# A decode step of two attention layers and two MLPs on one core: the tile of layer 1's exponentials, split maxima, a power for 1/deviation, and a new written-out order

## Chip, cores and metric

One core of a Trainium2 chip runs the kernel. The time is that of one execution on the device in microseconds (us). The engines are PE (TensorE: matmuls, with PEld for its weight loads), DVE (VectorE), ACT (ScalarE), POOL (GpSimd) and SP (SyncE, which issues the loads here); each works through its own queue in order, and they meet at semaphores.

## What is computed

Eight batch rows, one token each. Attention A reads the last 1024 positions of the caches (16 query heads on 8 key heads of 256), MLP B has 1792 hidden columns; the pair is run twice with the same weights and caches.

```python
def _A_ref(x, k_cache, v_cache, wq, wo):
    W = min(4096, max(256, Sk // 4))                  # 1024
    q = (x @ wq).reshape(B, Sq, Hq, Dh)               # heads first
    k = jnp.repeat(k_cache[:, :, Sk - W:, :], rep, axis=1)
    v = jnp.repeat(v_cache[:, :, Sk - W:, :], rep, axis=1)
    p = _softmax(jnp.einsum("bhqd,bhkd->bhqk", q, k) * Dh ** -0.5, axis=-1)
    o = jnp.einsum("bhqk,bhkd->bhqd", p, v)
    return o.reshape(B, Sq, Hq * Dh) @ wo
def _B_ref(x, w1, w2):
    return jnp.einsum("bsf,fd->bsd", _silu(jnp.einsum("bsd,df->bsf", x, w1)), w2)
x = x + _A_ref(_layernorm(x), ...)     # layer 1
x = x + _B_ref(_layernorm(x), w1, w2)
x = x + _A_ref(_layernorm(x), ...)     # layer 2, same wq, wo and caches
x = x + _B_ref(_layernorm(x), w1, w2)
```

## The kernel before

**Loads.** The weights are loaded once and stay. K and V pass through `ring`, 30 slots of one key head of one batch row (0.52 MB, loaded as two half slots of 256 KB). A row takes 16 slots, 8 of K and 8 of V, and both layers use them while they are there: layer 2 of a row needs what layer 1 and the MLP made of it, so K waits in its slots for layer 2's scores (which free four K slots for each half of the heads), and V for layer 2's products (`pv_rows` with layer 1 as its index). SP issues the loads in the order of the rows, each when its slot is free and at most ten ahead (`load_k` L713, `load_v` L719).

**One row, layer 1** (`layer1(b)`). DVE transposes the 16 half slots of K in place (L1246, called K transposes here). `q_blocks1` (L858, ACT) writes the row's queries into the tile `qbd[0]` as blocks with zeros between them, so that one matmul serves several heads. `scores` (L881) multiplies K by them into a PSUM bank; `softmax` takes the maximum (L892, DVE), turns it over the partitions (L900 to L905), and ACT makes exponentials with it as a bias (L912) into `e_sb`; PE transposes them (L918, ACT evicts at L927), sums them (L931), multiplies V (`pv_rows`, L951) into two banks for heads 0 to 7 and 8 to 15, of which ACT evicts each (L956) for a transposing matmul (L958) and DVE scales it (L971). One head group of V takes a column form (`pv_cols`, L985). `rows_part` (L1002) multiplies by wo in rows, ACT evicts the sum (L1018) and `fold` (L1019) adds it to the residual columns in bank YB.

**The MLP** (`up`, `chain`). ACT copies the residual to bf16 (L1029, L1030), `stat` (L1036, L1040) sums x and its square, DVE makes the variance (L1046), and `rsqrt` makes 1/deviation from it: a guess from the bits (L749) and two Newton steps (L754 and L760, or L757 to L765). `w1_rows` (L842) multiplies by w1, DVE transposes the result (L851) and subtracts the mean (L1063, `vt`), ACT makes the tanh (L1071, `th`), DVE the other factor (L1072, `zh`) and the product `hT` (L1074). w2 follows, by rows (L1002) and, for chunks from `nr` on, by columns (`cols_part`, L1008).

**Layer 2** (`chain`, `layer2(b)`). wq is multiplied in rows (L1104), DVE transposes that (L1109), PE selects heads and positions (L1115, called the selection), DVE adds the mean's share (L1121) and multiplies by a mask into `qbd[1]` (L1129), once for each half of the heads. Layer 2's `stat` hands its variance (L1051, ACT) to nine small POOL instructions (L749 to L765). Then come scores, softmax and V as in layer 1, while layer 1 of the next row runs in between. All of layer 2's outputs meet in `final` (from L1141), a second MLP for all eight rows at once.

**The order.** Each operation is recorded as a task with what it reads and writes. `best_schedule` runs a list scheduler with a model of durations, adds fixed offsets to the tasks' ranks (`OFFSETS`), runs it again and then moves single tasks by a table (`MOVES`). The scheduler also puts `fill` tasks into PE's gaps: matmuls of zeros by 512 columns (L1290) which change nothing. `PAIR0 = 1` lets layer 1's scores take both halves of the heads in one matmul of 512 columns, `NR2 = 14` sends all of w2 by rows (in the last row 8 chunks by rows), and `WQS = 0` keeps the first wq product in one bank (in the last row it goes to two).

**Tiles that the change touches.** `e_sb[0]`, `e_sb[1]`, `rowb`, `yT` and `o_sb[0]` all lie in the tile `qT`, which also takes the q transposes: layer 1's exponentials of a row cannot be written before the selection of the row before has read `qT`. The columns of `rowb` behind the 448 are zeroed by POOL in each row (L1257).

Of the kernel before, what the change touches and what calls it, by code (L numbers as in the profile page):

```python
# [1 line left out]

# [12 lines left out]
SEM_LAT = {"pe": 0.05, "dve": 0.05, "act": 0.05, "pool": 0.08, "sp": 0.1}  # L15
LAT = {"pe": 0.17, "dve": 0.07, "act": 0.09, "pool": 0.08, "sp": 0.0}
SWITCH = 0.1
FETCH = (128, 1.4, 0.26)
WINDOW, WARM, ACTIVE, PACED = 3.413, 43.0, 3072.0, 50.0
FIRST, LANDED = 1.2, 1.5  # L20
HOLDS = (("PVc0", 1, "oTc0", 1), ("s12", 1, "hT", 1), ("wq", 2, "qbd", 1))
HELD = ("KT", "max0")
OFFSETS = (
# [26 lines left out]
)  # L50
LOOKS = (0.3, 0.15)

MOVES = {
# [1275 lines left out]
```

## Time and profile before

| | us |
|---|---|
| three runs: median (lowest, highest) | 241.06 (241.04, 242.05) |
| the profiled execution: span from first to last instruction | 239.7 |
| what the median has over that span | 1.36 |
| PE busy, all matmuls; of this fillers (L1290, 129 matmuls) | 194.1; 38.6 |
| DVE busy; of this K transposes (L1246, 128) | 152.8; 81.4 |
| ACT busy; POOL busy | 86.5; 26.0 |
| last stretch, 206 us to the end: DMA | 4 GB/s |

The profile is of one execution, and durations are from it. A line of the groups gives line, engine, operation, out<-in, count, then busy time, mean of one in ns, and the idle time of the engine just before them with what ended it. A line of the timeline gives start, length, engine, line and operation. In the chain of waits each piece has its start and the time that it alone held the end up. "x16" behind a matmul is a count.

### The profile page before, as it was taken

Reading aid. Unit: us, or ns where it says so; the run is one execution under the profiler, and the core shown is the slowest. Engines: PE = TensorE matmul, PEld = TensorE weight load, DVE = VectorE, ACT = ScalarE, POOL = GpSimd, SP = SyncE. Lnnn points to the kernel's source line nnn. Section 1 sums busy time; section 2 is a strip of 40 time slices with the busy share of each in tenths; the row PEclk is TensorE's granted clock in tenths of the full one; section 3 lists DMA queues with packets and bytes.
Section 4 is the critical chain, followed back from the end, with each engine's and each line's share of the span. In section 5 each row is a group of like instructions: output and inputs, shape, how many; then the busy total and the mean of one; then the engine's idle time right before and its main releaser. Section 6 shows DMA issues by size and latency. Waiting matters only on the chain.

```text
span 239.7 us, 8472 instructions
## 1 busy us (share of the span) xinstructions
PE 194.1 (81%) x3567; PEld 97.3 (41%) x3567; DVE 152.8 (64%) x425; ACT 86.5 (36%) x292; POOL 26.0 (11%) x125
## 2 busy tenths in 40 slices
PE   1052358878989899989898898989898999899894
PEld 1051123232345344535433453454344535445552
DVE  7339620037955995996599669946985996334533
ACT  2001231033045516532734354355416440544331
POOL 6100000002010031004001200310031003003000
PEclk9999985999999999999999999999999999999999
DMA  6999999999999999999999999999999999200000
GB/s 228 373 355 403 404 402 384 378 374 406 402 405 403 403 402 404 398 350 379 360 400 402 371 373 379 376 368 377 358 399 399 397 330 399 102 3 3 4 3 1
DMA packets 40341, 78.22 MB, mean 326 GB/s; under 512 B 4320, under 2 KB 6512, under 8 KB 39792
## 3 DMA queue, kind: packets, MB, share of 16 engines
q1 hardware_dynamic: 40304, 77.69, 87.2%
q8 instruction: 28, 0.46, 0.7%
q14 instruction: 9, 0.07, 0.1%
HBM read 77.67 MB, written 0.01 MB: 324 GB/s over the span
## 4 chain that ended last, share of the span: by engine, by line
PE 47%; DMA 19%; DVE 16%; ACT 7%; SPq 7%; issue 4%; POOL 0%; DVEq 0%; ACTq 0%
DMA ring<-in_A_k_cache_dram 10%; PE bank L951 9%; PE bank L881 7%; DMA w2o<-in_B_w_dram 6%; DVE ring L1246 6%; PE bank L1002 6%; PE bank L1290 5%; PE bank L1104 5%; PE bank L1115 3%; DMA ring<-in_A_v_cache_dram 3%; SPq L682 3%; ACT qT L912 2%; DVE mrow L892 2%; PE bank L918 2%; PE bank L958 1%
## 5 line engine op out<-in xcount | busy, mean ns | idle before, releaser
L1246 DVE STREAM_TRANSPOSE ring<-ring 128x512 uint32<-128x512 uint32 x128 | 81.4, 684 | 10.7 <-DMA ring<-in_A_k_cache_dram 10.7
L1290 PE MATMUL bank<-wq_sb,smalls 128*128 128x512 bf16 x129 | 38.6, 386 | 0.0
L881 PE MATMUL bank<-ring,qbd 128*16 128x512 bf16 (+2 forms) x768 | 35.8, 324 | 3.4 <-DVE ring L1246 2.3
L951 PE MATMUL bank<-ring,pT_sb 128*4 128x512 bf16 (+1 forms) x512 | 36.2, 378 | 0.1
L881 PEld LDWEIGHTS bank<-ring,qbd 128*16 128x16 bf16 (+1 forms) x768 | 19.6, 91 | 17.1 <-DVE qbd L1129 3.9
L858 ACT ACTIVATE qbd<-q1s 32x128 bf16<-32x128 bf16 x32 | 10.2, 320 | 42.9 <-PE bank L881 42.3
L892 DVE TENSOR_REDUCE mrow<-bank 128x2 f32<-128x512 f32 (+1 forms) x17 | 11.0, 646 | 11.9 <-PE bank L881 11.1
L1104 PE MATMUL bank<-wq_sb,xn 128*4 128x512 bf16 (+1 forms) x272 | 17.7, 369 | 0.9 <-ACT x2s L1091 0.5
L1018 ACT ACTIVATE qT<-bank 128x448 bf16<-128x448 f32 x16 | 8.7, 543 | 22.4 <-PE bank L1002 22.4
L951 PEld LDWEIGHTS bank<-ring,pT_sb 128*4 128x4 bf16 (+1 forms) x512 | 11.5, 84 | 11.1 <-issue 1.8
L1290 PEld LDWEIGHTS bank<-wq_sb,smalls 128*128 128x128 bf16 x129 | 10.2, 98 | 12.3 <-issue 7.6
L918 PE MATMUL bank<-ident,qT 128*64 128x16 bf16 x256 | 8.5, 180 | 7.3 <-ACT qT L912 6.6
L1002 PE MATMUL bank<-w2o,oT 128*1 128x448 bf16 x224 | 13.2, 352 | 0.7 <-DMA w2o<-in_A_wo_dram 0.7
L956 ACT ACTIVATE qT<-bank 128x512 bf16<-128x512 f32 x16 | 9.6, 597 | 9.7 <-PE bank L951 6.7
L1109 DVE STREAM_TRANSPOSE qT<-bank 128x512 f32<-128x512 f32 (+1 forms) x17 | 11.3, 664 | 2.2 <-PE bank L1104 2.0
L918 PEld LDWEIGHTS bank<-ident,qT 128*64 128x64 bf16 x256 | 6.1, 111 | 12.5 <-ACT qT L912 11.5
L956 ACT ACTIVATE qbd<-bank 128x512 bf16<-128x512 f32 (+1 forms) x16 | 9.1, 570 | 5.5 <-PE bank L951 3.3
L749 POOL TENSOR_SCALAR smalls<-smalls 128x1 int32<-128x1 int32 x8 | 1.5, 190 | 86.9 <-ACT smalls L1051 76.3
L1257 POOL MEMSET qT<- 128x64 bf16 x8 | 1.2, 152 | 82.5 <-PE bank L958 68.7
L1115 PE MATMUL bank<-qT,w2o 128*32 128x64 f32 x128 | 8.4, 352 | 2.0 <-DVE qT L1109 0.8
L912 ACT ACTIVATE qT<-bank,mrow 128x256 bf16<-128x256 f32 x17 | 7.2, 470 | 7.6 <-DVE mrow L905 7.3
L1046 DVE SCALAR_TENSOR_TENSOR smalls<-bank,smalls 128x1 f32<-128x1 f32 x8 | 1.1, 143 | 13.2 <-ACT smalls L1044 9.5
(183 smaller groups left out, 254.6 us busy)
## 6 DMA issues: line engine op xcount, KB each, us to landing
ring<-in_A_k_cache_dram SPq DMA_DIRECT2D x128, 256.0 KB, 6.2
ring<-in_A_v_cache_dram SPq DMA_DIRECT2D x128, 256.0 KB, 6.1
w2o<-in_A_wo_dram SPq DMA_DIRECT2D x2, 1792.0 KB, 13.1
wq_sb<-in_A_wq_dram SPq DMA_DIRECT2D x3, 1024.0 KB, 6.8
w2o<-in_B_w_dram SPq DMA_DIRECT2D x1, 1568.0 KB, 14.5
w_sb<-in_B_w_dram SPq DMA_DIRECT2D x3, 448.0 KB, 12.2
wq_sb<-in_A_wq_dram SPq DMA_DIRECT2D x2, 256.0 KB, 10.2
w_sb<-in_B_w_dram SPq DMA_DIRECT2D x2, 112.0 KB, 11.4
```

Source lines behind the costliest of these rows:

```text
L881: fns.append(lambda e, cb=cb, par=par, j=j, kv=kv, m=m, c0=c0, c1=c1: e.matmul(bank[sc][32 * j:32 * j + m, c0:c1], qbd[layer][:, j * 8 + c ...
L892: dve(lambda e: e.tensor_reduce(mseg[layer][:, ks[0]:ks[-1] + 1], bank[sc][:, lo:hi].rearrange("p (k n) -> p k n", k=len(ks)), AX.X, ALU.m ...
L912: act(lambda e, k2=k2: e.activation(e_sb[ei][:, k2, :, :].rearrange("p uh (jj ul) -> p uh jj ul", ul=2), bank[sc][:, k2 * 256:(k2 + 1) * 2 ...
L918: pe([lambda e, uh=uh, ql=ql, k2=k2: e.matmul(bank[lb][64 * ql:64 * ql + 64, k2 * 64:k2 * 64 + 64].rearrange("p (j q u r) -> p u j q r", j ...
L951: fns.append(lambda e, qh=qh, uh=uh, j=j, vv=vv: e.matmul(bank[ob][32 * j:32 * j + 2 * w, 0:w * DH], p_col(ei, k2, j, qh, uh, w), vv, star ...
L956: act(lambda e: e.activation(o_sb[oi][:, 0:w * DH], bank[ob][:, 0:w * DH], ACTF.Copy), bk(ob), O_K[oi], 0.2 + w * 0.2, "oevh" if ob == OB[ ...
L1002: pe([lambda e, i=i, c=c: e.matmul(bank[XB][32 * c:32 * c + 1, 0:D], rhs(i), w_sb[:, i * D:(i + 1) * D], start=(first and i - i0 < 4), sto ...
L1104: fns.append(lambda e, j=j, c=c, wb=wb, off=off, h0=h0, n=n, k2=k2: e.matmul(bank[wb][32 * j:32 * j + 4, h0:h0 + n], xn[:, part(c, k2), j, :],
L1109: dve(lambda e, wb=wb, h0=h0, n=n: e.transpose(qT[:, h0:h0 + n].rearrange("p (c a i) -> p c a i", a=2, i=32), bank[wb][:, h0:h0 + n].rearr ...
L1115: pe([lambda e, qs=qs, j=j: e.matmul(qs[32 * j:32 * j + 32].rearrange("p (k c r) -> p k r c", k=4, c=8), irep, qT[:].rearrange("p (r c i) ...
L1246: dve(lambda e, v=v: e.transpose(v, v), [("slot", s, h)], [("slot", s, h)], 0.67, "KT")
L1290: fills = {n: [lambda e, j=j, m=P // n: e.matmul(bank[OB[0]][m * j:m * j + m, 0:2 * DH], zero_b.broadcast_to([P, m]), wq_sb[:, 0:2 * DH], ...
```

## The change

1. `e_sb[0]` and `o_sb[0]` move from `qT` to `qbd[0]`, layer 1's own query tile. POOL zeroes it in each row but the last, behind the zeroing of `rowb`, and ACT writes the next row's queries after that.
2. Layer 1's maximum is taken for each half of the heads by itself, and its scores too (`PAIR0 = 0`): 64 matmuls of 256 columns a row in place of 32 of 512.
3. 1/deviation of each row's two layer norms is one POOL instruction, variance to the power -0.5; the variance changes its sign and loses the factor of the Newton steps. Layer 2's variance is made on DVE in place of ACT. `zh` moves from DVE to POOL. The Newton steps stay at the start and in `final`.
4. `NR2 = 8`: 6 chunks of w2 go by columns in every row. `WQS = 1`: the first wq product goes to two banks by halves in every row. The second query addition uses `pT_sb[1]` as its buffer (in the last row `mrow[0]` as before).
5. The scheduler, its tables and its model are gone; `ORDER` holds each engine's order as numbers of tasks, with fillers as f1, f2 and f4 (that many matmuls; f2 and f4 use 64 or 32 columns of the array each). 50 filler matmuls in 17 places are left of 129.

```diff
-    NJ, PAIR0, PAIR1, NR2, WQS = 3, 1, 0, 14, 0
+    NJ, PAIR0, PAIR1, NR2, WQS = 3, 0, 0, 8, 1
...
-    e_sb = [qT[:, 256 * i:256 * i + 256].bitcast(BF16).rearrange("p (k u x) -> p k u x", k=2, u=4) for i in range(2)]
+    e_sb = [t.rearrange("p (k u x) -> p k u x", k=2, u=4) for t in (
+        qbd[0][:].rearrange("p n k x -> p (n k x)"), qT[:, 256:512].bitcast(BF16))]
+    QB1 = [("qbq", 0, q) for q in range(4)]
...
-    o_sb = [qT[:, 0:256].bitcast(BF16), qbd[1][:].rearrange("p n k x -> p (n k x)")]
+    o_sb = [q[:].rearrange("p n k x -> p (n k x)") for q in qbd]
...
+    mhalf = smalls[:, 14:15]
...
-        row_max(layer, ks, sc)
+        for k in ((0,), (1,)) if layer == 0 else (ks,):
+            row_max(layer, k, sc)
...
-            dve(lambda e: e.scalar_tensor_tensor(out=va, in0=t2, scalar=-kk / D, in1=m2, op0=ALU.mult,
-                                                 op1=ALU.add), bk(bi) + ["m2"], [("va", si)], 0.16, "va")
+            dve(lambda e: e.scalar_tensor_tensor(out=va, in0=t2, scalar=kk / D, in1=m2, op0=ALU.mult,
+                                                 op1=ALU.subtract), bk(bi) + ["m2"], [("va", si)], 0.16, "va")
...
-            act(lambda e: e.activation(va, t2, ACTF.Identity, bias=m2[:, 0:1], scale=-kk / D), bk(bi) + ["m2"],
-                [("va", si)], 0.26, "va")
-        rsqrt(dve if si == 0 else pool, va, rstd, nt, ("va", si), ("rstd", si), [])
+        pool(lambda e: e.tensor_tensor(rstd, va, mhalf, ALU.pow), [("va", si), "mhalf"], [("rstd", si)], 0.54, "pow")
...
-        dve(lambda e: e.tensor_scalar(zh[:], vt[:], rstds[0][:, 0:1], None, op0=ALU.mult), ["vt", ("rstd", 0)],
-            ["zh"], 0.234, "zh")
+        pool(lambda e: e.tensor_scalar(zh[:], vt[:], rstds[0][:, 0:1], None, op0=ALU.mult), ["vt", ("rstd", 0)],
+             ["zh"], 0.25, "zh")
...
+        if b < NB - 1:
+            pool(lambda e: e.memset(qbd[0][:], 0.0), [], QB1 + [("qbd", 0, 0), ("qbd", 0, 1)], 0.52, "qz")
...
-    pl.best_schedule(fill)
+    pl.arrange(ORDER, fills, "oevh")
```

Three places of the order, each as it was and as it is now. First PE, from row 3's first selection on (before: L1115 is the selection, L1104 the wq product, L881 scores: 8x256 and 16x256 of layer 2 for row 3, 16x512 of layer 1 for row 4, L997 starts row 4's residual):

```order
L1115 MATMUL bank<-qT,w2o 32x4x2x8 x4
L997 MATMUL bank<-xb,ident 128x64
L1104 MATMUL bank<-wq_sb,xn 4x512 x16
L881 MATMUL bank<-ring,qbd 8x256 x32
L1290 MATMUL bank<-wq_sb,smalls 128x512
L881 MATMUL bank<-ring,qbd 16x512 x8
L1115 MATMUL bank<-qT,w2o 32x4x2x8 x4
L881 MATMUL bank<-ring,qbd 16x512 x24
L881 MATMUL bank<-ring,qbd 16x256 x32
```

The same stretch of row 3 now, from its fold (L797) on; L658 are scores, L884 the wq product, L814 and L818 the statistics, L895 the selection:

```order
L797 MATMUL bank<-smalls,qT 128x16 x4
L658 MATMUL bank<-ring,qbd 8x256 x24
L884 MATMUL bank<-wq_sb,xn 4x256 x32
L658 MATMUL bank<-ring,qbd 8x256 x8
L814 MATMUL bank<-xbt 128x32 x4
L818 MATMUL bank<-smalls 128x16
L895 MATMUL bank<-qT,w2o 32x4x2x8 x4
L884 MATMUL bank<-wq_sb,xn 4x512 x16
L658 MATMUL bank<-ring,qbd 8x256 x32
L658 MATMUL bank<-ring,qbd 16x256 x24
L895 MATMUL bank<-qT,w2o 32x4x2x8 x4
L658 MATMUL bank<-ring,qbd 16x256 x8
```

Of layer 1's scores for row 4, 24 + 8 matmuls of the first half stand before the first selection and 24 of the second half before the second one (the 8x256 x32 between are layer 2's of row 3); 8 are left behind it. The statistics have moved behind the halves of the wq product.

Second DVE at the same place, from row 3's first q transpose (L1109) to the maximum (L892), before:

```order
L1109 STREAM_TRANSPOSE qT<-bank 128x512
L1246 STREAM_TRANSPOSE ring<-ring 128x512
L1121 TENSOR_TENSOR mrow<-bank,mrow 128x64
L1129 TENSOR_TENSOR qbd<-mrow,smalls 128x32x8
L1246 STREAM_TRANSPOSE ring<-ring 128x512 x2
L1109 STREAM_TRANSPOSE qT<-bank 128x512
L1121 TENSOR_TENSOR mrow<-bank,mrow 128x64
L892 TENSOR_REDUCE mrow<-bank 128x2
```

And now (L889 q transposes, L829 the variance of layer 2, L1026 K transposes, L901 and L909 addition and mask, L669 the maxima):

```order
L889 STREAM_TRANSPOSE qT<-bank 128x256 x2
L829 SCALAR_TENSOR_TENSOR smalls<-bank,smalls 128x1
L1026 STREAM_TRANSPOSE ring<-ring 128x512
L901 TENSOR_TENSOR mrow<-bank,mrow 128x64
L909 TENSOR_TENSOR qbd<-mrow,smalls 128x32x8
L1026 STREAM_TRANSPOSE ring<-ring 128x512 x2
L889 STREAM_TRANSPOSE qT<-bank 128x512
L901 TENSOR_TENSOR pT_sb<-bank,pT_sb 128x64
L669 TENSOR_REDUCE mrow<-bank 128x1 x2
```

The first q transpose is two halves, a variance has come in, and the maximum is two instructions. In row 6 the two maxima stand behind L909 instead, ahead of the second q transpose.

Third POOL in a row, before (L1257 zeroes the end of `rowb`, L1129 masks the second half of layer 2's queries):

```order
L1257 MEMSET qT 128x64
L749 TENSOR_SCALAR smalls<-smalls 128x1
L757 TENSOR_TENSOR smalls<-smalls 128x1
L758 TENSOR_TENSOR smalls<-smalls 128x1
L763 TENSOR_SCALAR smalls<-smalls 128x1
L765 TENSOR_TENSOR smalls<-smalls 128x1
L757 TENSOR_TENSOR smalls<-smalls 128x1
L758 TENSOR_TENSOR smalls<-smalls 128x1
L763 TENSOR_SCALAR smalls<-smalls 128x1
L765 TENSOR_TENSOR smalls<-smalls 128x1
L1129 TENSOR_TENSOR qbd<-mrow,smalls 128x32x8
```

And now (L1039 zeroes the query tile, L831 are the two powers, L850 is `zh`):

```order
L1037 MEMSET qT 128x64
L1039 MEMSET qbd 128x512
L831 TENSOR_TENSOR smalls<-smalls 128x1
L850 TENSOR_SCALAR zh<-vt,smalls 128x14
L831 TENSOR_TENSOR smalls<-smalls 128x1
L909 TENSOR_TENSOR qbd<-pT_sb,smalls 128x32x8
```

Nine instructions of layer 2's Newton steps have become one power, and the power and `zh` of the MLP between layers have come in ahead of it.

More of the change, by code (lines that the diff above doesn't have):

```diff
@@ new lines, in arrange @@
+    def arrange(self, table, fills, reader):
+        work = [t for t in self.tasks if t.eng != "sp"]
+        loads = [t for t in self.tasks if t.eng == "sp"]
+        self.order = {e: [] for e in ("pe", "dve", "act", "pool")}
+        reads = {}
+        for t in self.tasks:
+            if t.name == reader:
+                reads.update((o.idx, t) for o, _ in t.deps.values() if o.name.startswith("PV0"))
+        for e in self.order:
+            last = None
+            for word in table[e].split():
+                if word[0] == "f":
+                    n, _, after = word[1:].partition("@")
+                    t = Task("pe", fills[int(n)], 0.2, 0.0, "fill")
+                    t.idx, t.sem, t.shape = len(self.tasks), None, (512, int(n))
+                    for k in ("zero_b", ("bank", 2)):
+                        t.deps[self.first_w[k].idx] = (self.first_w[k], True)
+                    if last:
+                        t.deps[last.idx] = (last, False)
+                    if after:
+                        t.deps[loads[int(after)].idx] = (loads[int(after)], True)
+                    self.tasks.append(t)
+                    self.order[e].append(t)
+                    continue
+                lo, _, hi = word.partition("-")
+                for i in range(int(lo), int(hi or lo) + 1):
+                    self.order[e].append(work[i])
+                    last = reads.get(work[i].idx, last)
+        self.order["sp"] = loads
+        assert sum(len(o) for o in self.order.values()) == len(self.tasks)
@@ L861, in q_blocks1 @@
                 [("q1s", t), ("qbd", 0, 0), ("qbd", 0, 1)], [("qbq", 0, q)], 0.3, "qbd1")
-    QB1 = [("qbq", 0, q) for q in range(4)]
     def scores(b, layer, ks, sc):
@@ L924, in softmax @@
                 start=True, stop=True, tile_position=(0, 64 * ql)) for uh in range(4) for ql in range(2)],
[L925 removed]
+               E_K[ei][k2] + ["ident"], bk(lb), (16, 2), "pT%d" % layer)
         k0, k1 = ks[0], ks[-1] + 1
@@ L1129, in chain @@
             (pool if k2 and not tail else dve)(lambda e, dst=dst, qb=qb, mk=mk: e.tensor_tensor(dst, qb, mk, ALU.mult),
-                                               QF + mkey, [("qbd", 1, k2)], 0.55 if k2 and not tail else 0.4, "qbd")
+                                               QF[k2] + mkey, [("qbd", 1, k2)], 0.55 if k2 and not tail else 0.4, "qbd")
     def rows8(banks, n, w_sb, rhs, reads, name):
```

293 lines of the change are left out of this document (30 added, 263 removed), and 89 rows, old and new, of tables (MOVES, OFFSETS, ORDER).

## Prediction

> **What bounds the kernel now.** I read the page first: the span, the rate of the loads over 40 slices, and the chain that ended last.
>
> ```profile
> span 239.7 us, 8472 instructions
> GB/s 228 373 355 403 404 402 384 378 374 406 402 405 403 403 402 404 398 350 379 360 400 402 371 373 379 376 368 377 358 399 399 397 330 399 102 3 3 4 3 1
> PE 47%; DMA 19%; DVE 16%; ACT 7%; SPq 7%; issue 4%; POOL 0%; DVEq 0%; ACTq 0%
> ```
>
> The loads run until slice 34, some 205 us, and 33 us of work follow. They reach 403 to 406 GB/s but do not hold it. The view by stretches of time puts a border on that (columns: stretch, length, busy time of PE, PEld, DVE, ACT and POOL, granted clock, DMA share, GB/s).
>
> ```profile
> 54.00:102.00 48.00, 43.86 (x761) 20.64 (x765) 37.42 (x87) 18.90 (x65) 5.22 (x22) 1.00 1.05 403
> 102.00:196.00 94.00, 85.28 (x1617) 42.03 (x1609) 73.14 (x198) 42.55 (x144) 10.42 (x44) 1.00 1.03 376
> ```
>
> Until 102 us the loads set the pace: a batch row brings 32 half slots of 0.262 MB, 8.39 MB, which at 403 GB/s is **20.8 us a row** (0.65 us a half slot). After 102 us they get only 376 GB/s, since slots of the ring come free late: there the work of a row is the longer. To measure a row I take the transpose behind the w1 product (L851), once a row. The timeline shows it for rows 2, 6 and 7.
>
> ```profile
> 102.89 0.65 DVE L851 STREAM_TRANSPOSE qT<-bank 128x448 f32<-128x448 f32 x1
> 191.98 0.65 DVE L851 STREAM_TRANSPOSE qT<-bank 128x448 f32<-128x448 f32 x1
> 213.15 0.64 DVE L851 STREAM_TRANSPOSE qT<-bank 128x448 f32<-128x448 f32 x1
> ```
>
> Rows 2 to 6 take (191.98 - 102.89) / 4 = **22.27 us** each, row 6 to 7 takes 21.17, and 26.55 us follow to the end. So a row stands 1.5 us over the pace of the loads. Where these go is read from the chain of waits in row 3 (start, length, what):
>
> ```profile
> 126.23 0.92 PE bank L1002 x14
> ...
> 127.79 0.27 PE bank L1019 x4
> ...
> 128.55 1.03 PE bank L1104 x16
> 129.59 0.20 PE bank L1036 x4
> 129.79 0.03 PE bank L1040
> ...
> 130.70 0.53 PE bank L1115 x6
> ...
> 132.33 0.89 PE bank L881 x30
> ...
> 134.08 0.34 PE bank L1115 x4
> 134.42 1.41 PE bank L881 x20
> ...
> 135.85 0.70 DVE mrow L892
> ```
>
> The w2 product, its fold (L1019), the q product (L1104), the selection (L1115), and the scores (L881): behind the second selection stand 1.41 us of layer 1 scores of the next row, which do not need that selection at all, and only then its maximum (L892).
>
> **The change, step by step.** Sizes first: the page of groups has the column form of the w2 product, and the view by source line has both forms of the maximum (minimum, median, longest in ns).
>
> ```profile
> L1008 PE MATMUL bank<-hT,w2o 128*128 128x16 bf16 x24 | 0.7, 170 | 0.0
> L1018 ACT ACTIVATE qT<-bank 128x448 bf16<-128x448 f32 x16 | 8.7, 543 | 22.4 <-PE bank L1002 22.4
> L892 DVE TENSOR_REDUCE mrow<-bank x17: 425/691/693, 31.5 to 224.0; 128x2 f32<-128x512 f32 x15, 128x1 f32<-128x256 f32 x2
> ```
>
> 1. Layer 1 scores come in 64 matmuls of 256 columns instead of 32 of 512, in 8 groups of 8; a group takes 8 x 0.89 / 30 = 0.24. Seven stand ahead of the second selection, one behind. From the selection's end to the end of the maximum it was 1.41 + 0.02 + 0.70 = 2.13. Now the last group lies beside the add on DVE, then two half maxima follow, 0.25 + 2 x 0.425 + two hops of 0.05 = 1.2: **-0.9**.
> 2. The w2 product keeps 8 of 14 chunks as rows, 0.92 x 8 / 14 = 0.53; the other 6 as 24 column matmuls (0.7) lie beside the eviction (0.543). Product to fold was 127.79 - 126.23 = 1.56; now 0.53 + 0.7 + 0.05 = 1.3: **-0.25**.
> 3. Three score groups (0.72) are put between fold and q product, where 128.55 - 128.06 = 0.49 lay open for the copies on ACT: **+0.2**.
> 4. The first q product goes to two banks as halves, so that half the transpose lies beside the second half. Product to selection was 130.70 - 128.55 = 2.15, some of it waiting for DVE; now 1.03, one score group 0.24, the statistics' matmuls (L1036 and L1040) 0.23 and some hops, 1.7: **-0.45**.
>
> Together -1.4, which would make a row 20.9. The second selection I leave where it is: behind the masked queries PE has 32 + 24 score matmuls (1.7), before it had 32, a filler and 8 long ones (134.08 - 132.33 = 1.75).
>
> Powers: POOL takes over 1/deviation. For layer 2 nine POOL instructions become one; for layer 1 five DVE instructions become one on POOL, between the variance (L1046) and the tanh, which waits also for L1063. From the timeline, the layer 2 sequence's ends and the layer 1 slack in row 3:
>
> ```profile
> 123.92 0.16 DVE L1046 SCALAR_TENSOR_TENSOR smalls<-bank,smalls 128x1 f32<-128x1 f32 x1 [0.17 <-PE bank L842]
> 125.31 0.24 DVE L1063 SCALAR_TENSOR_TENSOR vt<-cs,smalls,qT 128x14 f32<-128x14 f32 x1
> 130.65 0.19 POOL L749 TENSOR_SCALAR smalls<-smalls 128x1 int32<-128x1 int32 x1 [10.54 <-ACT x2s L1091]
> 132.96 0.19 POOL L765 TENSOR_TENSOR smalls<-smalls 128x1 f32<-128x1 f32 x1
> ```
>
> No row shows a power. Below it is one POOL instruction on one column, 0.19; above the whole sequence that it replaces, 133.15 - 130.65 = 2.5. The slack is 125.55 - 124.08 = 1.47, less two hops 1.3. I take about 0.5, near the one instruction: cost 0, hidden by the transpose L851. Without that cover each us above 1.3 costs 1 us a row. The product zh goes to POOL beside the tanh.
>
> ```profile
> L1072 DVE TENSOR_SCALAR zh<-vt,smalls 128x14 f32<-128x14 f32 x8 | 1.7, 217 | 0.2
> L1071 ACT ACTIVATE th<-vt,smalls 128x14 f32<-128x14 f32 x8 | 2.5, 307 | 9.0 <-DVE smalls L760 8.8 <-DVE vt L1063 0.2
> ```
>
> It has 0.307 of cover and POOL's small instructions take about 0.2: cost 0. The Trainium skill, GPSIMD Engine Reference, section Key points, calls the vector engine about twice as fast in elementwise work; by that an estimate is 0.43, which would show 0.13 in each of 8 rows, 1.0 us in all; the POOL rows above, as short as DVE's, speak against it at this size.
>
> The query tile of layer 1 now holds exponentials and outputs, so it must be zeroed and rebuilt before the next row's scores:
>
> ```profile
> L626 POOL MEMSET qbd<- 128x512 bf16 x2 | 1.0, 524 | 0.1
> L858 ACT ACTIVATE qbd<-q1s 32x128 bf16<-32x128 bf16 x32 | 10.2, 320 | 42.9 <-PE bank L881 42.3
> 119.95 0.15 POOL L1257 MEMSET qT<- 128x64 bf16 x1 [6.89 <-ACT pT_sb L927]
> ```
>
> The memset follows the one at 119.95, done by 120.7; four copies of 0.32 in gaps of ACT are done by about 124, two to four us before the first scores are asked for (126 to 128). Cost 0; if a copy stands in front of an eviction it costs 0.3. The loads, from DVE's timeline and from the view of waits of SP's queue (waited in all, times, longest):
>
> ```profile
> 95.73 1.35 DVE L1246 STREAM_TRANSPOSE ring<-ring 128x512 uint32<-128x512 uint32 x2 [0.45 <-DMA ring<-in_A_k_cache_dram]
> 98.54 3.67 DVE L1246 STREAM_TRANSPOSE ring<-ring 128x512 uint32<-128x512 uint32 x6
> SPq L719 <- PE bank L881: 8.6, 5, 1.9
> ```
>
> In row 2 nine K transposes stand ahead of L1046 in both orders, and the first waits for its data at 95.73. The ninth lands at 95.73 + 8 x 0.65 = 100.9; with its transpose and the variance, L851 cannot start before 101.75. So all that is gained earlier (the maximum of row 1 need not wait for the first row's second selection) comes to 102.89 - 101.75: **-1.1**.
>
> For rows 2 to 6 I do not take 20.9, on the floor of the loads, but **21.4**: the K transposes wait for loads now, stand in DVE's queue ahead of L851 and the q transposes, and hold them a few tenths a row; layer 2's variance, moved from ACT, stands there too (0.16, as L1046). On PE the early score groups wait for eight of these transposes, and behind them in its queue stand the q product (in rows 4 and 5 the w2 product too), so that a late load now stops the row itself. 4 x (22.27 - 21.4): **-3.5**.
>
> Row 6 to 7: layer 1's maximum of row 7 now stands right behind the first masked query product of row 6, not behind the second.
>
> ```profile
> 198.51 0.42 DVE L1129 TENSOR_TENSOR qbd<-mrow,smalls 128x256 bf16<-128x256 f32 x1
> 202.32 0.69 DVE L892 TENSOR_REDUCE mrow<-bank 128x2 f32<-128x512 f32 x1 [1.05 <-PE bank L881]
> ```
>
> L851 to that product's end was 198.93 - 191.98 = 6.95, less 0.5 of steps 2 to 4, and two half maxima, 0.9: 7.35. From the maximum's end to the next L851 was 213.15 - 203.01 = 10.14; 32 scores of row 6 (1.0) now stand between the two V products, and the last V slots, which SP loads only after the scores of row 6 (the L719 row: longest wait 1.9), I take as 1 us late: 12.2. Sum 19.6 against 21.17: **-1.6**. The tail of 26.55 keeps its chain: 0.
>
> Sum: 239.7 - 1.1 - 3.5 - 1.6 = 233.5. The three runs have a median of 241.06, 1.36 over the span: **234.9 us**.
>
> **Rivals.** (a) The floor: rows at 20.8, 4 x 0.6 less: 232.5. Speaking for it are 403 GB/s until 102 us; against it the queues that now wait for loads. (b) The ring: slots are freed by layer 2's scores, which now end later against the maximum, so rows stay at 22.27 and the first and last terms alone stay: 238.4. (c) The clock. PE's fillers (L1290) fall from 129 matmuls to 50, in 17 places. Early on, before the fillers, the stretches read:
>
> ```profile
> 31.09:34.51 3.42, 0.98 (x25) 0.44 (x18) 1.29 (x4) 2.12 (x7) 0.00 (x0) 1.00 1.05 401
> 34.51:37.92 3.41, 2.71 (x31) 0.93 (x34) 0.43 (x2) 0.86 (x2) 0.00 (x0) 0.50 1.05 397
> 41.33:44.74 3.41, 3.07 (x14) 1.17 (x12) 0.00 (x0) 0.00 (x0) 0.00 (x0) 1.00 1.06 399
> ```
>
> After 3.4 us with PE busy for 0.98 the granted clock is 0.50. If one such stretch a row comes back, PE's 47% of the chain, 1.6 us of it, runs at half speed and loses 0.8: 7 rows, +5.6, 240.5. Against it: scores and V products fill the gaps that fillers filled. The Trainium skill, TensorE: Matmul & The Clock Gate, section What's actually happening, has the clock halved after an idle stretch of some 3.4 us and full again after a busy one, on a window that runs freely; the trace agrees (0.98 of 3.42 busy, then 0.50). (d) Slower: the power is long. At 2.5 us it is 1.2 over the slack, 8 rows, +9.6: 244.5. From 2.1 us on, 0.8 x 8 = 6.4, the gain is gone; beyond 2.2 the kernel is slower.
>
> **How the numbers follow.** Forecast 0.42 (233 to 237.5), (a) 0.18, (b) 0.14, (c) 0.16, (d) 0.07, and 0.03 for a stall that I have not seen, slower. About 0.5% (239.85 to 242.27) can be told from no change. Faster: forecast, (a), (b) and a few hundredths of (c), 0.76. Same: most of (c), 0.12. Slower: (d), the unseen, 0.12 with the bad end of (c). The range, 231 to 241.5, holds (a), (b) and nearly all of (c); it leaves out (d).
>
> **What would show it.** Steps 1 to 4: after 102 us about 392 GB/s (8.39 MB in 21.4), and the transposes behind the w1 product 21.4 apart. Step 1: the half maxima right behind the second add. Powers: POOL's instruction under 1.3 us, and ACT's tanh released by vt, not by POOL. Clock: 1.00 in every slice after 41 us. It is wrong if rows stay over 22, if POOL or DMA releases the tanh or PE's scores, or if the tail grows by more than 0.5.

## The result and the profile after

The changed kernel takes 240.85 us (median of nine runs, 238.94 to 243.51), the kernel before on the same chips 241.51 (nine runs, 241.04 to 242.13). The ratio is 0.9944, with a 95% interval of 0.9917 to 0.9971: a gain of 0.6% where 2.6% was forecast. (Here and below a ratio leaves out runs over 1.5% above the fastest of their kernel, here three of nine; a median does not.) The time forecast, 234.9, was missed by 6 us; the range, 231.0 to 241.5, holds the median.

The profiled execution took 238.94, the fastest of the nine. The traces below explain that one; what the median has above it, 1.9 us, no trace shows. Its page: the span, the granted clock and the load rate over 40 slices, and the chain that ended last, by engine and by line.

```profile
span 237.1 us, 9247 instructions
...
PEclk9999998875699999979999999999999999999997
...
GB/s 224 381 362 402 406 403 386 384 370 406 403 404 402 403 403 400 400 281 360 403 403 349 393 399 363 289 401 403 402 394 399 401 403 395 213 3 3 3 3 3
...
DMA 40%; PE 35%; DVE 13%; ACT 5%; SPq 4%; issue 3%; POOL 0%; DVEq 0%; ACTq 0%
DMA ring<-in_A_k_cache_dram 22%; DMA ring<-in_A_v_cache_dram 11%; PE bank L658 7%; DMA w2o<-in_A_wo_dram 7%; PE bank L729 6%; DVE ring L1026 6%; PE bank L884 4%; PE bank L780 4%; PE bank L621 2%; PE bank L786 2%; PE bank L895 2%; SPq L510 2%; PE bank L736 1%; PE bank L915 1%; PE bank L696 1%
```

Before, PE held 47% of the chain and DMA 19%; now DMA leads with 40%, a third of the whole chain being landings of K and V. Yet the loads are no faster: slices 17, 21 and 25, counted from 0, show 281, 349 and 289 GB/s. A queue that leads the chain while it moves less than it can is waiting for leave to work.

The transpose behind the w1 product, L851 of before, is now L630 (timeline of DVE, rows 2, 3, 6 and 7).

```profile
103.09 0.65 DVE L630 STREAM_TRANSPOSE qT<-bank 128x448 f32<-128x448 f32 x1 [0.49 <-PE bank L621]
125.44 0.65 DVE L630 STREAM_TRANSPOSE qT<-bank 128x448 f32<-128x448 f32 x1 [0.45 <-PE bank L621]
191.49 0.61 DVE L630 STREAM_TRANSPOSE qT<-bank 128x448 f32<-128x448 f32 x1
211.34 0.65 DVE L630 STREAM_TRANSPOSE qT<-bank 128x448 f32<-128x448 f32 x1 [0.49 <-PE bank L621]
```

Rows 2 to 6 now take (191.49 - 103.09) / 4 = 22.10 us, not 21.4; row 6 to 7 takes 19.85. Where the gain of a row went is seen when it is cut in three, at the first selection and at the first V product of the next row. In row 3, from PE's timeline:

```profile
131.29 0.53 PE L895 MATMUL bank<-qT,w2o 128*32 128x64 f32 x8 [0.58 <-DVE smalls L829]
...
138.54 1.03 PE L729 MATMUL bank<-ring,pT_sb 128*4 128x512 bf16 x16 [0.46 <-ACT pT_sb L705]
```

From L630 of row 3 the selection comes after 5.85 us (6.07 before), the V product 7.25 behind it (before 139.13 - 130.70 = 8.43), and the next L630, at 147.93, another 9.39 later (8.33 before). The same cuts as means of rows 2 to 5, read from the same rows of the timelines; the two lower lines belong to experiments below:

| us | w1 transpose to selection | to first V product | to next w1 transpose | row |
|---|---|---|---|---|
| before | 5.93 | 8.32 | 8.02 | 22.27 |
| changed | 5.90 | 6.97 | 9.22 | 22.10 |
| changed, wider ring | 5.84 | 6.93 | 8.41 | 21.18 |
| before, wider ring | 5.93 | 8.31 | 7.93 | 22.17 |

So 1.4 us a row were gained up to the V product, what the steps had summed to, and 1.2 were lost behind it. The view by stretches shows that last part of row 3, first before, then now (length, busy time of PE, PEld, DVE, ACT, POOL, clock, DMA share, GB/s):

```profile
139.13:147.46 8.33, 8.32 (x181) 4.20 (x178) 6.60 (x18) 4.26 (x12) 0.15 (x1) 1.00 1.04 383
```

```profile
138.54:147.93 9.39, 8.47 (x181) 4.31 (x185) 6.33 (x16) 5.42 (x16) 0.52 (x1) 1.00 1.02 382
```

The same 181 matmuls at the same clock: before, PE had no idle time here at all; now it has 0.92. The chain of waits names what it waits for (start, length, what):

```profile
132.68 1.03 PE bank L658 x32
133.71 0.02 issue
133.72 0.33 SPq L510
...
135.47 0.04 issue
135.52 6.42 DMA ring<-in_A_k_cache_dram
141.94 0.02 issue
141.96 1.90 DVE ring L1026 x3
143.86 0.07 DVE oT L749
143.92 0.04 issue
143.97 0.74 PE bank L780 x12
```

It is best read backwards. PE's wo product (L780) waits for an attention output on DVE (L749). That stands in DVE's queue behind K transposes of row 5 (L1026), and the first of them waits for its load, which lands 6.42 us after its issue. SP issues loads in the order of the ring, and ahead of this one stand loads of V (L510). They could go out only when PE had finished the first masked scores of row 3 (L658, 133.71), which free slots of the ring. The load that waits for these scores goes out 8.4 us behind the w1 transpose in both kernels (rows 2 to 5: 8.43, 8.64, 8.19 and 8.38 before, 8.65, 8.28, 8.34 and 8.37 now), since nothing ahead of the first selection became faster. What the change shortens lies behind that point, so the loads of a row start no earlier, and the gain runs into them.

### The profile page after: what moved, and what is told of

Its sections match the earlier page's. It is cut to its first block, busy times and chain, and to the rows that moved or that the text cites. A ratio compares the mean times of both kernels' runs of the same rounds, so it can differ in the third digit from the quotient of the medians.

```text
span 237.1 us, 9247 instructions
## 1 busy us (share of the span) xinstructions
PE 175.3 (74%) x3979; PEld 100.1 (42%) x3982; DVE 148.2 (62%) x400; ACT 86.0 (36%) x285; POOL 26.5 (11%) x85
## 4 chain that ended last, share of the span: by engine, by line
DMA 40%; PE 35%; DVE 13%; ACT 5%; SPq 4%; issue 3%; POOL 0%; DVEq 0%; ACTq 0%
DMA ring<-in_A_k_cache_dram 22%; DMA ring<-in_A_v_cache_dram 11%; PE bank L658 7%; DMA w2o<-in_A_wo_dram 7%; PE bank L729 6%; DVE ring L1026 6%; PE bank L884 4%; PE bank L780 4%; PE bank L621 2%; PE bank L786 2%; PE bank L895 2%; SPq L510 2%; PE bank L736 1%; PE bank L915 1%; PE bank L696 1%
## 5 line engine op out<-in xcount | busy, mean ns | idle before, releaser
L1026 DVE STREAM_TRANSPOSE ring<-ring 128x512 uint32<-128x512 uint32 x128 | 82.8, 688 | 15.3 <-DMA ring<-in_A_k_cache_dram 15.2
L658 PE MATMUL bank<-ring,qbd 128*8 128x256 bf16 (+1 forms) x1024 | 39.5, 283 | 8.5 <-POOL qbd L909 3.9
L658 PEld LDWEIGHTS bank<-ring,qbd 128*8 128x8 bf16 (+1 forms) x1024 | 23.7, 88 | 20.2 <-POOL qbd L909 6.4
L734 ACT ACTIVATE qbd<-bank 128x512 bf16<-128x512 f32 (+1 forms) x32 | 18.6, 580 | 15.3 <-PE bank L729 11.3
L884 PE MATMUL bank<-wq_sb,xn 128*4 128x256 bf16 (+1 forms) x384 | 20.3, 331 | 0.8 <-ACT smalls L822 0.2
L669 DVE TENSOR_REDUCE mrow<-bank 128x1 f32<-128x256 f32 (+1 forms) x25 | 11.9, 495 | 10.0 <-PE bank L658 10.0
L831 POOL TENSOR_TENSOR smalls<-smalls 128x1 f32<-128x1 f32 x16 | 8.9, 559 | 76.8 <-DVE smalls L824 39.9
L780 PE MATMUL bank<-w2o,oT 128*1 128x448 bf16 x224 | 14.0, 351 | 1.4 <-DVE oT L749 1.3
L889 DVE STREAM_TRANSPOSE qT<-bank 128x256 f32<-128x256 f32 (+1 forms) x24 | 12.1, 517 | 0.8 <-PE bank L884 0.7
L1039 POOL MEMSET qbd<- 128x512 bf16 x7 | 3.7, 525 | 75.9 <-PE bank L736 75.9
L749 DVE TENSOR_TENSOR oT<-bank,mrow 128x16 bf16<-128x16 f32 (+1 forms) x16 | 2.6, 161 | 14.9 <-PE bank L736 14.9
L884 PEld LDWEIGHTS bank<-wq_sb,xn 128*4 128x4 bf16 x384 | 8.9, 90 | 6.3 <-issue 1.2
L621 PE MATMUL bank<-w_sb,xbt 128*1 128x448 bf16 (+1 forms) x128 | 10.4, 398 | 1.1 <-issue 0.6
L637 ACT ACTIVATE qbd<-q1s 32x128 bf16<-32x128 bf16 x32 | 10.2, 319 | 2.9 <-POOL qbd L1039 2.1
L895 PE MATMUL bank<-qT,w2o 128*32 128x64 f32 x128 | 8.6, 350 | 1.9 <-DVE smalls L829 1.2
L555 PE MATMUL bank<-xb,smalls 128*128 128x8 bf16 x4 | 0.3, 173 | 11.9 <-DVE ring L552 11.9
L736 PE MATMUL bank<-ident,qbd 128*128 128x8 bf16 x124 | 8.2, 171 | 1.2 <-ACT qbd L734 0.9
```

The lines of the kernel that those rows point to most:

```text
L621: pe([lambda e, i=i, k=k, c=c: e.matmul(bank[bi][32 * c:32 * c + n, 0:FN], lhs(k), w1_sb[:, i * F + c * FN:i * F + (c + 1) * FN] if i < 3 else
L637: act(lambda e, q=q: e.activation(qbd[0][32 * q:32 * q + 32].rearrange("p n k (q r) -> p k n q r", r=2)[:, :, :, q, :], q1s[32 * t:32 * t ...
L658: fns.append(lambda e, cb=cb, par=par, j=j, kv=kv, m=m, c0=c0, c1=c1: e.matmul(bank[sc][32 * j:32 * j + m, c0:c1], qbd[layer][:, j * 8 + c ...
L669: dve(lambda e: e.tensor_reduce(mseg[layer][:, ks[0]:ks[-1] + 1], bank[sc][:, lo:hi].rearrange("p (k n) -> p k n", k=len(ks)), AX.X, ALU.m ...
L734: act(lambda e: e.activation(o_sb[oi][:, 0:w * DH], bank[ob][:, 0:w * DH], ACTF.Copy), bk(ob), O_K[oi], 0.2 + w * 0.2, "oevh" if ob == OB[ ...
L736: pe([lambda e, a=a, i=i: e.matmul(bank[lb][:, C_O + (k2 * 2 + a) * 8:C_O + (k2 * 2 + a) * 8 + 8], o_sb[oi][:, i * DH + a:(i + 1) * DH:2], ...
```

## Experiments

Three theories stood. **Theory 1 (ring):** slots come free at the old time, the loads land as late as before, and PE and DVE wait for them. **Theory 2 (queue):** the loads are in time, but the new order puts K transposes ahead of the attention outputs in DVE's queue. **Theory 3 (clock):** with 50 fillers for 129, PE falls to half clock too often.

**E1 and E2: half of the K loads almost empty from row 4 on, in both kernels.** The scores of these rows are then made from old data.

```diff
+            n = 1 if h and b >= 4 else P
-                e.dma_start(slots[s][:, 1024 * h:1024 * h + 1024], src[:, 1024 * h:1024 * h + 1024])
+                e.dma_start(slots[s][0:n, 1024 * h:1024 * h + 1024], src[0:n, 1024 * h:1024 * h + 1024])
```

> The changed kernel, but from row 4 on the second half of every K slot is loaded as one partition (2 KB) instead of 128 (256 KB), so that scores of those rows are computed on old data; every instruction, wait and queue place stays, only the landings come earlier. Theory 1 (ring): after the first masked scores free the slots (8.4 us behind the w1 transpose, before and after the change alike), the K halves land one every 0.65 to 0.7 us, and seven to nine of them have to be transposed ahead of the next w1 transpose; with four of these landing at once the rows up to row 6 fall from 22.1 to about 21, 4 x 1.1 = 4 to 5 us less than the changed kernel, near 236. Theory 2 (queue): the K transposes hold DVE's queue ahead of the attention outputs whether their data is there or not: at most 1 us less. Theory 3 (clock): no change.

> The kernel before with the same small loads of the second K halves from row 4 on. In its trace PE has no idle time between the first V product of a row and the next w1 transpose (7.84 of 7.84 us busy, 8.32 of 8.33). Theory 1 (ring): PE's own work sets its rows, so 0 to 1.5 us less, rows of 22; the two kernels then differ by 4 us or more, the gain that was forecast. Theory 2 (queue) and theory 3 (clock): no change, and the two kernels differ as before, by 0.6 to 2.5 us.

Measured: 236.53 us for the changed kernel (ratio to before 0.9815, 0.9751 to 0.9879), 241.18 for the one before (0.9996, 0.9975 to 1.0018). Earlier landings are worth 3 to 4 us to the new order (3.1 by the ratios 0.9944 and 0.9815, 4.3 between the medians) and nothing to the old one. Rows 2 to 6 of the changed kernel fall to 21.3, by the same transposes. This speaks against theory 2, and theory 3 foresaw no change. It doesn't yet say why the loads are late: fewer bytes would help a kernel that is held by their rate, too.

**E3: attention outputs ahead of K transposes, rows 2, 4 and 5.** DVE's order in row 2:

```diff
 L749 TENSOR_TENSOR oT<-bank,mrow 128x2x8
-L1026 STREAM_TRANSPOSE ring<-ring 128x512 x2
+L1026 STREAM_TRANSPOSE ring<-ring 128x512
 L749 TENSOR_TENSOR oT<-bank,mrow 128x2x6
-L1026 STREAM_TRANSPOSE ring<-ring 128x512 x3
+L1026 STREAM_TRANSPOSE ring<-ring 128x512
 L769 TENSOR_TENSOR oT<-bank,mrow 128x2x2
-L1026 STREAM_TRANSPOSE ring<-ring 128x512 x4
+L1026 STREAM_TRANSPOSE ring<-ring 128x512 x7
```

> The changed kernel with only DVE's order changed in rows 2, 4 and 5: the second and third attention output steps (L749 x12, L769) stand one to three K transposes earlier. Theory 2 (queue): PE's idle time for these steps, 0.9 to 1.2 us a row, goes: 2 to 3 us less than the changed kernel. Theory 1 (ring): the variance and the w1 transpose stand behind the same seven to nine K transposes, which end 0.65 us behind their landing, so only what is gained on the first scores counts: 0 to 1 us less. Theory 3 (clock): no change.

Measured: median 242.35, nine runs from 236.88 to 245.83, ratio 0.990 (0.985 to 0.995). The runs lie nine microseconds apart, and the interval overlaps that of the changed kernel (0.9917 to 0.9971). So the 2 to 3 us of theory 2 are neither shown nor excluded by this run alone.

**E4: the w1 transpose ahead of K transposes too.** DVE's order in row 2, behind the outputs, which lie as in E3 (six K transposes ahead of L824 instead of nine):

```diff
 L1026 STREAM_TRANSPOSE ring<-ring 128x512 x4
-L714 RECIPROCAL rl_sb<-bank 128x16
 L824 SCALAR_TENSOR_TENSOR smalls<-bank,smalls 128x1
 L630 STREAM_TRANSPOSE qT<-bank 128x2x224
 L841 SCALAR_TENSOR_TENSOR vt<-cs,smalls,qT 128x14
+L1026 STREAM_TRANSPOSE ring<-ring 128x512 x3
+L714 RECIPROCAL rl_sb<-bank 128x16
 L1026 STREAM_TRANSPOSE ring<-ring 128x512
 L852 SCALAR_TENSOR_TENSOR hT<-th,zh 128x14
```

> As the run before, and in rows 2 to 5 the layer 1 variance and the w1 transpose (L824, L630, L841) too stand two to four K transposes earlier. Theory 1 (ring): the w1 transpose no longer waits for the last landings, 0.7 to 1.2 us a row earlier, and the slots are freed that much earlier: 2 to 4 us less than the changed kernel, unless the first score groups, which wait for eight K halves, take the wait over (then 0 to 1). Theory 2 (queue): as the run before, 2 to 3 us less. Theory 3 (clock): no change.

Measured: 245.81, ratio 1.0141 (1.0069 to 1.0214). A miss for all theories, and partly an ill-made edit: in row 2 four K transposes, where one had been, came to stand between L841 and L852, which the w2 product waits for, and in row 3 PE waits 1.76 us for a reciprocal (L714) that now stands behind a K transpose. Row 3 in DVE's timeline, of an execution of 247.41 us, shows one more cost:

```profile
127.14 0.16 DVE L824 SCALAR_TENSOR_TENSOR smalls<-bank,smalls 128x1 f32<-128x1 f32 x1 [1.29 <-ACT smalls L822]
...
129.58 3.71 DVE L1026 STREAM_TRANSPOSE ring<-ring 128x512 uint32<-128x512 uint32 x6
```

DVE stands idle for 1.29 us in front of L824, with K transposes queued behind it that now run later; the score groups ahead of the q product wait for these. Here, moving work past a late load only moved the wait.

**E5: step 3 undone, the early score groups behind the first masked scores (rows 1 to 5).** PE's order in row 1; the groups are the `ring,qbd` rows of 256 columns:

```diff
 MATMUL bank<-smalls,qT 128x16 x4
-MATMUL bank<-ring,qbd 8x256 x16
 MATMUL bank<-xbt 128x32 x4
 MATMUL bank<-smalls 128x16
 MATMUL bank<-wq_sb,xn 4x256 x32
-MATMUL bank<-ring,qbd 8x256 x8
 MATMUL bank<-qT,w2o 32x4x2x8 x4
 MATMUL bank<-wq_sb,xn 4x512 x16
 MATMUL bank<-xb,ident 128x64
-MATMUL bank<-ring,qbd 8x256 x40
+MATMUL bank<-ring,qbd 8x256 x64
```

> The changed kernel with step 3 undone in rows 1 to 5: the score groups of the next row that stand around the w2 fold and the q product are put behind the first masked scores, ahead of the second selection, where the others are. Theory 1 (ring): the first masked scores free the slots up to 0.7 us earlier (8.4 us behind the w1 transpose becomes 7.7), the loads and with them the next w1 transpose follow, and what the maximum loses is covered by the 1.2 us for which PE waits behind the first V product: 1.5 to 3 us less than the changed kernel. Theory 2 (queue): the maximum comes 0.5 to 0.7 us later a row, so 1 to 3 us more. Theory 3 (clock): no change, or slower, since PE has larger gaps around the fold.

Measured: 242.19, ratio 1.0008 (0.996 to 1.0055). No gain, so the forecast drawn from theory 1 missed. Its premise was the fault: the first masked scores did not come 0.7 us earlier. In row 3 PE waits in the place of the score groups (PE's timeline):

```profile
129.30 1.12 PE L883 MATMUL bank<-wq_sb,xn 128*4 128x256 bf16 x32 [0.42 <-ACT xn L864]
```

The groups had been lying beside the copies on ACT. The loads that wait for the scores go out 8.18, 7.99 and 8.27 us behind the w1 transpose in rows 3 to 5, 0.2 earlier on average, and the maximum comes later. Step 3 costs the path about nothing.

**E6, E7 and E8: more fillers,** with the changed order, with that of E5, and with the loads of E1. An added row of PE, as it stands ahead of the wo rows:

```diff
+MATMUL bank<-wq_sb,smalls 32x512 x4
 MATMUL bank<-w2o,oT 1x448 x12
```

> The changed kernel with 19 more groups of four filler matmuls in rows 1 to 6: ahead of the last wo rows, the wo fold and the w2 rows, where PE waits. Theory 3 (clock): the half clock behind 100 us and the later ones that come in some runs go, the mean clock (0.915 to 0.962 in nine runs of the changed kernel) rises to 0.97 or more, the runs come together, and the median falls by 1.5 us or more, to 239 or less. Theory 1 (ring): the loads still set the rows, so the median falls by what the half clock costs in row 2 alone, 0.5 to 1 us, and the rows from 103 us on stay at 22. Theory 2 (queue): as theory 1.

> The two before together, with 24 filler groups. Theory 1 (ring): 2 to 4 us less than the changed kernel. Theory 2 (queue): 0 to 2 us more. Theory 3 (clock): 1.5 us less, as the fillers alone.

> The run with small loads of the second K halves from row 4 on (scores of those rows on old data), with the 19 filler groups. Theory 1 (ring) and theory 3 together: what the loads' landing and the half clock took from the forecast are both given back, so about 1 us under 236.5, near the 234.9 that was forecast. Theory 1 without theory 3: 236.5, no change. Theory 3 without theory 1 cannot be, since the small loads alone brought 4 us.

Measured: 241.83 (ratio 1.001, 0.9975 to 1.0045), 242.06 (1.0034, 1.0 to 1.0068) and 239.74 (0.9889, 0.984 to 0.9938). None is faster than its base, so what the fillers were expected to bring did not come. The page of E6 shows the clock:

```profile
PEclk9999998865688999999999999999999999999998
```

From slice 13, 78 us, it is full until the last slice, and yet rows 2 to 6 take 22.8 us each (w1 transposes at 103.38 and 194.76) and the span is 240.3: theory 3 is not what holds the changed kernel. Where the loads are out of the way, E8 lies 1.8 us above E1 by the ratios, with intervals that overlap: no gain there either.

**E9 and E10: the same bytes, with and without free slots.** Both leave out the loads of the eighth K head from row 3 on and let its transposes and scores work on another head's slot. E9 keeps its slot in the ring, E10 does not.

```diff
+    def kslot(b, k):
+        return slot_of[b, "k", (6 if b < 6 else 5) if k == 7 and b >= 3 else k]
 E9, the loads of that head:
+            n = 1 if kvh == 7 and b >= 3 else P
 E10:
-    seq = [(b, t, k) for b in range(NB) for t in "kv" for k in range(8)]
+    seq = [(b, t, k) for b in range(NB) for t in "kv" for k in range(8) if (t, k) != ("k", 7) or b < 3]
```

> The changed kernel, but from row 3 on the eighth K head is not loaded (its two loads move one partition each into its own slot), and transposes and scores of that head work on another head's slot (the sixth's or seventh's). The ring's order and the times at which its slots come free stay; 0.52 of 8.39 MB a row are gone, 1.3 us of loads at 403 GB/s. It is the base for the next run. Theory 1 (ring): SP's pauses behind the first masked scores stay, so rows stay near 21.5 to 22. If instead the rate of the loads itself sets the rows, they fall by up to 1.3 us a row here.

> The same, but from row 3 on the eighth K head has no loads and no slot at all: 30 slots then hold two rows of 15 instead of 1.9 rows of 16, and the loads that waited for the first masked scores wait for V products seven microseconds earlier. Bytes, transposes and scores are as in the run before. Theory 1 (ring): SP's pauses go and PE's own work sets the rows, about 21: 2 to 4 us less than the run before. If the rate of the loads sets the rows: equal to the run before within 0.5 us. Theory 2 (queue): equal.

Measured: E9 240.51 (ratio 0.9949, 0.991 to 0.9988), E10 **234.99** (0.9715, 0.9646 to 0.9785). With 0.52 MB less a row E9 is where the changed kernel is, rows of 22.17 us; the mean rate of the loads does not set its rows. (It does not test the first landings of a row: the half slots left out are the last two of a row's sixteen of K, and seven to nine stand ahead of the w1 transpose.) With the same bytes and more room in the ring the time falls by 5.5 us, more than the 2 to 4 that were expected. What SP's queue waits for (in all, times, longest; 103 to 185 us) shows it, first E9:

```profile
SPq L514 <- PE bank L662: 6.9, 4, 3.9
SPq L514 <- PE bank L899: 4.7, 2, 3.1
SPq L508 <- PE bank L733: 3.6, 4, 2.1
```

and E10, where the scores are L661, the selection L898 and the V product L732:

```profile
SPq L513 <- PE bank L732: 7.0, 3, 2.9
...
SPq L507 <- PE bank L661: 2.0, 2, 1.7
...
SPq L507 <- PE bank L898: 1.0, 1, 1.0
SPq L513 <- PE bank L898: 0.8, 1, 0.8
...
SPq L507 <- PE bank L732: 0.7, 2, 0.3
```

The pauses around the masked scores fall from 11.6 us to 3.8; those behind V products grow from 3.6 to 7.7. In all SP waits no less, 26.3 us against 23.7, but the loads are no longer late. In rows 2 to 6 loads hold 27% of the changed kernel's chain (14.7 for K, 12.7 for V), and DVE waits six times for a landing of K, 2.9 us in all. In these rows E10's chain has no load in it, and neither PE nor DVE waits for one. E10's rows 2 and 6, in DVE's timeline:

```profile
102.79 0.65 DVE L633 STREAM_TRANSPOSE qT<-bank 128x448 f32<-128x448 f32 x1
...
187.52 0.61 DVE L633 STREAM_TRANSPOSE qT<-bank 128x448 f32<-128x448 f32 x1
```

That is 21.18 us a row, and DVE's order is still that of the change: theory 2 is not needed. A small part of the difference to E9 is the clock: E9's profile has half clock for 3.4 us from 127.7, where its selection of row 3 came 6.87 us behind the w1 transpose (6.09 in E10), and E10 has full clock in all these rows. That is 0.8 of the 3.9 us by which rows 2 to 6 differ. Another 1.2 lie ahead of row 2's transpose, where E9 has half clock from 100.4; how much of them is the ring is open.

**E11: the fillers of before cut to 8 columns.**

```diff
-        bank[OB[0]][...], zero_b.broadcast_to([P, m]), wq_sb[:, 0:2 * DH]
+        bank[OB[0]][...], zero_b.broadcast_to([P, m]), wq_sb[:, 0:8]
```

> The kernel before with its 129 filler matmuls cut from 512 to 8 columns, all else and the order as it was. Theory 3 (clock): the clock falls from 1.00 to about the 0.95 of the changed kernel, half-clock stretches come back in rows 1 to 6 and the time rises by 2 us or more. Theory 1 (ring): the clock may fall, but what matters is small: PE gains the fillers' own time, so within 1 us of before.

Measured: 252.34, ratio 1.040 (1.031 to 1.0489). The profiled execution took 255.87, the longest of four; its clock:

```profile
PEclk9999975555779768899798979997978899999586
```

The other three, 250.76 to 253.23, have mean clocks of 0.934 to 0.956, as the changed kernel has; they left no trace. Theory 3 foresaw this for the kernel before, theory 1 did not. So at about the same mean clock the kernel before loses 4%, some 10 us, although its PE has 26 us of filler work less (38.6 us before, 12.5 in this profile). In that kernel PE leads the chain with 47%, which fits; that this is why half clock costs so much there is argued, not shown. The mechanism of rival (c) exists, and for the kernel before its price is higher than (c) had it.

**E12: the wider ring of E10 in the kernel before.** Its own order is kept, written out as a table in place of the scheduler. The edit is that of E10, with other stand-in slots for the eighth head, and the scratch tiles of the last step in other slots.

> The kernel before, in its own order of tasks, with the edit of the run with the wider ring: from row 3 on the eighth K head has no loads and no slot, and its transposes and scores work on another head's slot; the last step's scratch tiles lie in two other slots. Theory 1 (ring): PE's own work sets the rows of before (from the first V product to the w1 transpose it has no idle time), so it stays within 1.5 us of before, 240 to 242, and the changed kernel with the wider ring (234.99) lies 5 to 7 us under it, the 6.1 that were forecast. If the ring held the kernel before as well, it falls by 4 to 6 us like the changed one, to 236 or 237, and the change itself is then worth 1 to 2 us only.

Measured: 241.02, ratio 0.9969 (0.9932 to 1.0007), and its chain by engine:

```profile
PE 52%; DMA 17%; DVE 16%; ACT 8%; issue 4%; SPq 2%; POOL 0%; DVEq 0%; ACTq 0%
```

The old order does not use the room. With it the change is worth 241.02 - 234.99 = 6.0 us; without it, 0.7 between the medians.

## Why the prediction was wrong, point by point

**Rows 2 to 6, forecast -3.5, measured -0.7.** The sum of the steps was right, -1.38 a row up to the first V product against -1.4, but by other parts: the stretch of step 1, from the first selection to the V product, became 1.35 shorter instead of 0.9, and that of steps 2 to 4, up to the selection, 0.03 instead of 0.5. That these make up for each other is luck. The step that failed is the next one: "For rows 2 to 6 I do not take 20.9, on the floor of the loads, but 21.4". It held the loads to arrive as they had done, and set a few tenths aside for K transposes that wait. Experiments 9, 10 and 12 show in its place that the loads wait for slots, the slots for the first masked scores, and that these did not move. Of the 1.2 us a row that the stretch behind the V product lost (8.02 to 9.22), 0.8 come back with the wider ring (8.41). The other 0.4 stays; there PE is busy for 8.20 of 8.41 us (7.97 of 8.02 before), so over half of it is more work for PE, and the rest is open. The working had this bound for row 2 alone, where the ninth K landing held L851, and for all rows as rival (b), "slots freed later", 238.4 with a chance of 0.14. It named the right mechanism, though the slots are freed not later than before but at the same time. The profiled 238.94 lies beside it, the median does not.

With the ring out of the way the row measured 21.18. That the time of E10, 234.99, lies so near to 234.9 is partly luck: rows 2 to 6 fell by 4.4 us instead of 3.5, row 6 to 7 by 2.0 instead of 1.6, and row 2 by 0.1 instead of 1.1.

**Row 2, forecast -1.1, measured +0.2.** The bound itself was late: the ninth K half landed at 101.54 instead of 100.9, since the third had landed 1.4 us behind the second, and DVE was ready for L630 at 102.61 instead of 101.75. Then L630 waited 0.49 for the w1 product. The view by stretches, around it:

```profile
97.97:101.38 3.41, 2.34 (x60) 1.42 (x59) 3.41 (x7) 1.57 (x6) 0.00 (x0) 1.00 1.04 399
101.38:104.79 3.41, 3.30 (x37) 1.22 (x37) 2.86 (x9) 2.03 (x8) 0.88 (x2) 0.50 0.74 249
```

In the second stretch twelve w1 matmuls took 1.29 us, in row 4 at full clock 0.74 (PE's timeline).

```profile
101.72 1.29 PE L621 MATMUL bank<-w_sb,xbt 128*1 128x448 bf16 x12
...
146.90 0.74 PE L621 MATMUL bank<-w_sb,xbt 128*1 128x448 bf16 x12
```

This is rival (c), in one row instead of seven. They also started late: one of the query copies (L637) stands between the two copies of the residual on ACT (L807 and L808), and the statistics ahead of the product wait for the second. From the chain of waits:

```profile
100.83 0.32 ACT qbd L637
```

Either one alone would have cost 0.15 at most, by these durations (an estimate): the product would have ended near 102.6, when DVE was ready.

**Row 6 to 7, forecast -1.6, measured -1.3:** near, by terms of which one makes up for part of the other. The maximum of row 7 ended 8.0 us behind L630 (198.73 + 0.75 - 191.49) and not 7.35, since steps 2 to 4 gave nothing here either (the first selection came after 6.05, before after 5.67); the rest took 11.9 and not 12.2, and no engine waited for the V loads that were taken as 1 us late. **The tail, forecast 0, measured -0.8:** from 211.34 to the end 25.76 instead of 26.55. Row 7's own stretch up to the w1 transpose of `final` (233.40 before, 229.80 now) is 1.8 shorter, the rest 1.0 longer. There the variance and its Newton steps had begun 0.8 us ahead of that transpose and now begin 0.7 behind it, so part of both figures is a change of places. The half clock from 234.5 cost nothing: the last w2 product and what follows take 3.89 us, before 3.95. The four terms give 239.7 + 0.2 - 0.7 - 1.3 - 0.8 = 237.1.

**Power and zh on POOL, cost 0:** nearly right. From POOL's groups:

```profile
L831 POOL TENSOR_TENSOR smalls<-smalls 128x1 f32<-128x1 f32 x16 | 8.9, 559 | 76.8 <-DVE smalls L824 39.9 <-DVE smalls L829 36.9
...
L850 POOL TENSOR_SCALAR zh<-vt,smalls 128x14 f32<-128x14 f32 x8 | 2.7, 332 | 6.8 <-DVE vt L841 6.8
```

The power took 0.56, near the 0.5 taken and far below the slack of 1.3. The product zh took 0.332 where DVE had taken 0.217: my reading of POOL's rows, "as short as DVE's", was off. The Trainium skill, GPSIMD Engine Reference, section Key points, has the vector engine about twice as fast in elementwise work; the trace has 1.5 times. Beside the tanh it shows less than 0.1 a row (in row 3 it ends at 126.80, the tanh at 126.72). The memset stayed hidden, as taken. The query copies did not in every row: one stands in the chain of row 2, shown above, and two in row 4, 0.66 us, ahead of the square of the mean (L822), for which DVE waited 0.17.

**The signs.** Rows stayed over 22 (22.10). The loads ran at 379 GB/s in rows 2 to 6, as before, and not at 392. PE's scores were released by POOL, another sign of being wrong: four times in these rows, 2.0 us in all, they waited for the mask of the second half (L909), since 8 scores stand behind the second selection where 24 longer ones had stood. E10 has 2.1 us of the same wait and rows of 21.18, so this did not decide the result. The tanh was released by vt, as expected.

## What to carry to other kernels

When a ring of buffers feeds a loop, ask for each gain on which side it lies of the event that frees the slots: work that is shortened behind that event starts no load earlier, and the loop's period stays. An engine without idle time in a stretch says that loads are in time at the present pace only, not at the one that is hoped for. To tell late leave from low rate, run the same bytes once with and once without a spare slot.

## What was not expected of the hardware

The stretch from 97.97 us had PE busy for 2.34 of 3.41 us, and half clock followed. An earlier stretch of the same run, with 2.29, was followed by full clock:

```profile
67.25:70.66 3.41, 2.29 (x72) 1.46 (x60) 1.99 (x7) 0.89 (x3) 0.76 (x2) 1.00 1.06 405
70.66:74.07 3.41, 2.94 (x53) 1.45 (x57) 1.71 (x7) 2.24 (x6) 0.00 (x0) 1.00 1.04 398
```

So PE's busy time over such a stretch, as the profile counts it, did not tell which way the clock went. The Trainium skill, TensorE: Matmul & The Clock Gate, section What's actually happening, speaks of an idle window of this length; here one that was two thirds busy was enough once and not enough another time, and what decides between the two is open.

A low mean clock alone says little of the time. E10 has 0.953, most of its half clock lies between 40 and 65 us, where the loads set the pace, and it is the fastest of all. From 47 to 65 us the changed kernel has a mean clock of 0.62 and the kernel before 1.00, with loads at 387 and 386 GB/s; yet it reaches the w1 transpose of row 1 at 79.41 us, no later than the other (79.94).
